# One warm matmul, one weight copy and the order of the last outputs, in a fused FFT and GEGLU kernel

## The chip, the cores and the metric

One core of one Trainium2 chip. The metric is the device time of one execution in microseconds (us). A "run" is one such execution; each run also has the span from its first to its last instruction and the mean clock that TensorE was granted (1.0 is full speed). The device time is about 2 us longer than the span (616.80 against 614.9 us in before's profiled run). Quoted times are medians of runs.

## The reference

```
x: [8, 3008, 256] float32;  w_gate, w_val: [256, 1536];  w_out: [1536, 256]
X = fft(fft(x, axis=1), axis=2).real          # over the sequence, then the 256 features
t = X.reshape(24064, 256)
g = t @ w_gate
out = (gelu(g) * (t @ w_val)) @ w_out         # exact gelu (erf), float32
```

## The kernel before

The feature FFT is folded into the weights on the chip (`make_w` multiplies the gate and value weights by DFT matrices into `W_sb`). The sequence FFT is two stages of small matmuls. Its real part is even in the sequence index up to the sign of an odd part O, so each position gives two outputs: sign 0 ("even": E + O) and sign 1 ("odd": E - O). Two copies of a weight serve this: O, and -2 O, which turns E + O in PSUM into E - O. Layer 1 and gelu make two products h per piece of 128 of the 1536 features; layer 2 multiplies the twelve pieces by `w_out`.

Part A sits in the opening. "Warm" matmuls on zeros keep TensorE busy while the first data is prepared:

```python
def warm(n):                                            # L843
    ps = psum("o")
    for _ in range(n):
        nc.tensor.matmul(ps[:, :], idle[:, 0:128], idle[:, :], start=True, stop=True)
# ... cut ...
s1(0, 2, 0)()                       # stage 1, pair by pair; each needs a fold by VectorE
s1(0, 2, 1)()
t_sin()
gelu_table()
warm(6)
fold_piece(5, 4)
s1(0, 1, 0)()
s1(0, 1, 1)()
fold_piece(0, 1)
fold_piece(1, 4)
s1(0, 3, 0)()
s1(0, 3, 1, "V")()
warm(1)
s1(0, 0, 0)()
s1(0, 0, 1, "V")()
```

Part B sits in `make_w`, which copies the product out of PSUM and then writes the -2 O copy on the engine named, by default the engine of the first copy:

```python
if m_engine == "P":
    nc.gpsimd.tensor_scalar(dst, W["gv"[i], "O"][:, f0 : f0 + n], keep2, None, op0=ALU.mult)
elif (m_engine or engine) == "A":
    nc.scalar.activation(dst, src, AF.Copy, scale=keep2)              # L475
else:
    nc.vector.tensor_scalar(dst, src, keep2, None, op0=ALU.mult)      # L477
# ... cut; the plan, slot 2 of the first chunk:
(2, make_w(0, 512, 512, (0,), "V")), (2, make_w(0, 512, 512, (1,))),
```

Part C sits in the last layer 2. Its chunk has 481 positions: four groups ("sub") of 128, 128, 128 and 97, each with two signs, so eight outputs of twelve matmuls each. Each output is copied out of PSUM into a tile `out_sb` of its own, and then stored in two transfers:

```python
def osb_tile():
    return work([128, 2, C], FP32, "osb", 3, "out_sb")          # three buffers rotate
# ... cut; l2_piece, in the last chunk:
osb = osb_tile()
if sign == 0:
    nc.vector.tensor_copy(osb[:m, 0, :], pso[:m, half])                  # L791
    store(b, ci, sub, 0, osb[:, 0, :], nc.sync)
else:
    nc.scalar.activation(osb[:m, 1, :], pso[:m, half], AF.Copy)          # L794
    store(b, ci, sub, 1, osb[:, 1, :], nc.scalar)
# ... cut; store(): the first of two transfers goes to the named queue, the second to SyncE's
(nc.sync if i else queue).dma_start(out=dst, in_=...)                    # L675
# ... cut; the order:
subs = [nsub - 1, *range(nsub - 1)] if last(ci) else range(nsub)
l2s = [l2_piece(ci, s, g, f) for s in subs for g in range(2) for f in range(0, NFC, L2P)]
```

## Time and profile before

| before | |
|---|---|
| time, three runs | 616.60, 616.64, 617.27 us |
| span and granted clock of the profiled run | 614.9 us, 0.997 |
| TensorE busy | 98% of the span |
| TensorE's share of the chain that ended last | 94% |

A profile line of the chain is "start, length, link". A line of the timeline is "start, busy time, engine, source line, operation, output<-inputs, count", and in brackets how long the engine had been idle and whose end released it.

### The profile page before, as it was taken

How to read it: one execution, taken by the hardware profiler on the slowest of the kernel's cores; microseconds unless marked ns; L12 is line 12 of the kernel's file. 1: busy time of each engine (PE TensorE's matmuls, PEld its weight loads, DVE VectorE, ACT ScalarE, POOL GpSimd, SP SyncE). 2: the span in 40 equal slices, each digit the busy share in tenths (PEclk: the TensorE clock that was granted, in tenths of full speed). 3: DMA queues.
4: the chain of work that ended last, by engine and by line, in shares of the span. 5: the costliest groups of instructions: out<-in, count | busy, mean ns of one | idle time of the engine just before them, and what ended most of it. 6: DMA issues, size and time to landing. Idle time of an engine off the chain costs nothing.

```text
span 614.9 us, 12747 instructions
## 1 busy us (share of the span) xinstructions
PE 605.4 (98%) x4181; PEld 406.9 (66%) x4229; DVE 577.3 (94%) x941; ACT 425.0 (69%) x824; POOL 508.9 (83%) x513
## 2 busy tenths in 40 slices
PE   8999999999999999999999999999999999999997
PEld 4466666666666666666666666666666666666666
DVE  8799999999999999999999999999999999999992
ACT  6888677777776777667766677666776676666661
POOL 8999899999987999789997899869997655565551
PEclk8999999999999999999999999999999999999999
DMA  9962834547253364532553344533213223111123
GB/s 175 200 137 57 237 95 117 141 116 189 80 144 92 100 163 119 140 100 58 157 150 94 106 107 107 146 102 100 64 49 77 62 87 78 42 46 47 37 51 83
DMA packets 52466, 65.40 MB, mean 106 GB/s; under 512 B 7629, under 2 KB 47278, under 8 KB 50004
## 3 DMA queue, kind: packets, MB, share of 16 engines
q1 hardware_dynamic: 45472, 49.03, 30.5%
q0 software_dynamic: 6608, 15.29, 11.7%
q8 instruction: 33, 0.54, 0.4%
q10 hardware_dynamic: 320, 0.26, 0.2%
q14 instruction: 33, 0.27, 0.2%
HBM read 39.65 MB, written 30.17 MB: 114 GB/s over the span
## 4 chain that ended last, share of the span: by engine, by line
PE 94%; DVE 2%; issue 1%; DMA 1%; ACT 1%; SPq 1%; POOL 0%; DVEq 0%; POOLq 0%; ACTq 0%
PE ps_o L778 39%; PE ps_g L681 29%; PE ps_v L681 20%; PE ps_dft L562 2%; PE ps_dft L598 2%; DMA out_dram<-out_sb 1%; PE ps_dft L451 1%; SPq L675 1%; PE ps_o L847 0%; PE ps_dft L542 0%; ACT gelu_sb L705 0%; ACT gelu_sb L714 0%; DVE v_sb L751 0%; POOL h_sb L753 0%; PE ps_dft L603 0%
## 5 line engine op out<-in xcount | busy, mean ns | idle before, releaser
L753 POOL TENSOR_TENSOR h_sb<-gelu_sb,v_sb 128x512 bf16<-128x512 bf16 (+1 forms) x280 | 319.9, 1147 | 87.0 <-DVE v_sb L751 79.0
L778 PE MATMUL ps_o<-Wo_sb,h_sb 128*128 128x256 bf16 (+1 forms) x2232 | 334.3, 272 | 0.0
L778 PEld LDWEIGHTS <-h_sb 128*128 128x128 bf16 (+1 forms) x2304 | 228.6, 100 | 111.2 <-POOL h_sb L753 1.0
L733 DVE SCALAR_TENSOR_TENSOR ve_sb<-EB_sb,yw,ps_v 128x512 f32<-128x512 bf16 (+1 forms) x280 | 206.3, 737 | 18.6 <-PE ps_v L681 16.6
L705 ACT ACTIVATE gelu_sb<-ps_g 128x512 bf16<-128x512 f32 (+1 forms) x288 | 169.3, 588 | 78.1 <-PE ps_g L681 62.9
L749 DVE TENSOR_TENSOR h_sb<-gelu_sb,ps_v 128x512 bf16<-128x512 bf16 (+1 forms) x280 | 190.0, 678 | 0.7
L681 PEld LDWEIGHTS <-W_sb 128*128 128x128 bf16 x1440 | 138.4, 98 | 78.0 <-issue 1.7
L751 DVE SCALAR_TENSOR_TENSOR v_sb<-ve_sb,ps_v 128x512 f32<-128x512 f32 (+1 forms) x280 | 187.4, 669 | 0.0
L714 ACT ACTIVATE gelu_sb<-ps_g 128x512 bf16<-128x512 f32 (+1 forms) x288 | 168.6, 585 | 0.0
L681 PE MATMUL ps_g<-O_sb,W_sb 128*128 128x512 bf16 (+1 forms) x530 | 159.1, 374 | 2.7 <-DVE O_sb L610 0.3
L681 PE MATMUL ps_g<-E_sb,W_sb 128*128 128x512 bf16 (+1 forms) x287 | 107.6, 375 | 0.7 <-ACT gelu_sb L714 0.5
L681 PE MATMUL ps_v<-O_sb,W_sb 128*128 128x512 bf16 (+1 forms) x288 | 108.0, 375 | 0.0
L681 PE MATMUL ps_v<-E_sb,W_sb 128*128 128x512 bf16 (+1 forms) x288 | 107.9, 375 | 0.0
L798 ACT ACTIVATE out_sb<-ps_o 128x512 f32<-128x512 f32 x92 | 55.0, 598 | 34.2 <-PE ps_o L778 34.1
L229 POOL TENSOR_TENSOR eo_sb<-ab_sb 94x512 bf16<-94x512 f32 (+1 forms) x70 | 77.7, 1112 | 0.4
L565 ACT ACTIVATE S_sb<-ps_dft 96x512 bf16<-96x512 f32 x56 | 33.2, 592 | 29.7 <-PE ps_dft L562 29.7
L222 POOL TENSOR_TENSOR ab_sb<-x_raw,x_raw 94x508 f32<-94x508 f32 (+1 forms) x30 | 33.0, 1101 | 0.0
L225 POOL TENSOR_TENSOR ab_sb<-x_raw,x_raw 94x508 f32<-94x508 f32 (+1 forms) x30 | 33.0, 1100 | 0.0
L562 PE MATMUL ps_dft<-eo_sb,G 94*96 94x256 bf16 x119 | 22.3, 272 | 0.0
L608 ACT ACTIVATE E_sb<-ps_dft 128x512 bf16<-128x512 f32 (+1 forms) x23 | 13.6, 590 | 12.0 <-PE ps_dft L598 12.0
L608 ACT ACTIVATE O_sb<-ps_dft 128x512 bf16<-128x512 f32 (+1 forms) x22 | 13.0, 590 | 11.6 <-PE ps_dft L598 11.1
L163 POOL DMA_INDIRECT x_raw<-in_x_dram,idx x18 | 17.2, 957 | 2.9 <-issue 0.8
(151 smaller groups left out, 207.6 us busy)
## 6 DMA issues: line engine op xcount, KB each, us to landing
out_dram<-out_sb SPq DMA_DIRECT2D x364, 64.0 KB
x_raw<-in_x_dram SPq DMA_DIRECT2D x10, 768.0 KB
Z_sb<-z SPq DMA_DIRECT2D x7, 768.0 KB
z<-S_sb SPq DMA_DIRECT2D x7, 576.0 KB
EB_sb<-yrow SPq DMA_DIRECT2D x6, 376.2 KB
z<-S_sb SPq DMA_DIRECT2D x7, 192.0 KB
x_raw<-in_x_dram SPq DMA_DIRECT2D x2, 640.0 KB
x_stage<-in_x_dram SPq DMA_DIRECT2D x1, 768.0 KB
```

What stands on the lines that cost most here:

```text
L229: eng.tensor_tensor(_sub(eo, [[C, nj], [1, 128]], j0 * C + g * 128), ab(0, 0, [[1, 128]]), ab(1, 0, [[1, 128]]), op=op)
L562: nc.tensor.matmul(ps[:96, q * C : (q + 1) * C], G[:, j, :], _sub(eo, [[1, C]], j * C), start=(j == js[0]), stop=(j == js[-1]))
L565: nc.scalar.activation(_sub(st["S"], [[1, 512]], (4 * jg + 2 * half) * C, part_num=96), ps[:96, :], AF.Copy)
L681: nc.tensor.matmul(ps[:, :n], W[nm, part][:, fs], src, start=start, stop=stop, **kw)
L705: nc.scalar.activation(gl[:, 0, :n], pg[:, :n], AF.Gelu)
L714: nc.scalar.activation(_sub(gl, [[-1, n]], TOK + n - 1), pg[:, :n], AF.Gelu)
L733: nc.vector.scalar_tensor_tensor(ve[:, :n], EB_bufs[b][:, c0 : c0 + n], yw[:, fc : fc + 1], pv[:, :n], op0=ALU.mult, op1=ALU.add)
L749: nc.vector.tensor_tensor(st["h"][:, fc, 0, :n], gl[:, 0, :n], pv[:, :n], op=ALU.mult)
L751: nc.vector.scalar_tensor_tensor(_sub(vv, [[-1, n]], n - 1), ve[:, :n], 2.0, pv[:, :n], op0=ALU.mult, op1=ALU.subtract)
L753: nc.gpsimd.tensor_tensor(st["h"][:, fc, 1, :n], gl[:, 1, :n], vv[:, :n], op=ALU.mult)
L778: nc.tensor.matmul(pso[:m, half], st["h"][:, fc, sign, h0 : h0 + m], Wo_sb[:, fc, :], start=(fc == 0 and not (first and sign)), stop=(fc = ...
L798: nc.scalar.activation(_sub(osb, [[1, 2 * C]], 0, part_num=m), pso[:m, :], AF.Copy)
```

## The change

Its intent: take three waits off TensorE at the two ends of the program. A drops the warm matmul that stands ahead of stage 1's last pair (and issues two weight copies in a slightly different place, which leaves every engine's own sequence as it was). B moves one -2 O copy from ScalarE, where two gelus wait behind it, to VectorE. C computes two even outputs first in the last layer 2, so that the first odd output no longer waits for GpSimd's last product.

```diff
-            subs = [nsub - 1, *range(nsub - 1)] if last(ci) else range(nsub)
-            l2s = [l2_piece(ci, s, g, f) for s in subs for g in range(2) for f in range(0, NFC, L2P)]
+            order = [(s, g) for s in range(nsub) for g in range(2)]
+            if last(ci):
+                order = [(nsub - 1, 0), (0, 0), (nsub - 1, 1), *order[1:-2]]
+            l2s = [l2_piece(ci, s, g, f) for s, g in order for f in range(0, NFC, L2P)]
 ...
-        warm(1)
         s1(0, 0, 0)()
 ...
-        copies.pop()()
         make_w(1, 0, 256, m_at=minus, m_engine="V", tag="v", copy_at=copies)()
+        copies[0]()
 ...
-        copies.pop()()
+        copies[1]()
 ...
-                (2, make_w(0, 512, 512, (0,), "V")), (2, make_w(0, 512, 512, (1,))),
+                (2, make_w(0, 512, 512, (0,), "V")), (2, make_w(0, 512, 512, (1,), m_engine="V")),
```

## The prediction

> **What bounds the kernel now.** I read the page's busy table first, then its chain of work that ended last, then the chain and timeline of two stretches where TensorE is not the only link: 13 to 26 us and 599 us to the end.
>
> ```profile
> PE 605.4 (98%) x4181; PEld 406.9 (66%) x4229; DVE 577.3 (94%) x941; ACT 425.0 (69%) x824; POOL 508.9 (83%) x513
> ...
> PE 94%; DVE 2%; issue 1%; DMA 1%; ACT 1%; SPq 1%; POOL 0%; DVEq 0%; POOLq 0%; ACTq 0%
> ```
>
> TensorE carries 94% of the chain. Start-to-start distances of its matmuls agree: between 45 and 599 us the time beyond each matmul's own cadence sums to about 1.8 us (leaving out doubled distances of one lone matmul each, which are missing records). So a microsecond taken from a TensorE stall before 45 us should move all that follows, to the end. The change touches none of the steady state, only the two ends. The chain of waits of 0 to 45 us:
>
> ```profile
> 13.21 0.40 PE ps_dft L520 x5
> 13.61 0.34 PE ps_o L847
> 13.96 0.17 PE ps_g L520 x4
> ...
> 22.48 0.88 PE ps_dft L451 x4
> 23.36 0.02 issue
> 23.38 0.60 ACT W_sb L459
> 23.98 0.58 ACT W_sb L475
> 24.56 0.49 ACT gelu_sb L705
> 25.05 0.50 ACT gelu_sb L714
> 25.54 0.04 issue
> 25.58 0.81 PE ps_g L681 x3
> ```
>
> Columns: start, length, link. The warm matmul (L847) is itself a link of 0.34 us. At 23.38 the chain leaves TensorE for four ScalarE instructions; the second, L475, is the -2 O copy of the weight that the change moves. The timeline at the end:
>
> ```profile
> 600.45 2.24 POOL L753 TENSOR_TENSOR h_sb<-gelu_sb,v_sb 128x481 bf16<-128x481 bf16 x2 [0.78 <-DVE v_sb L751]
> ...
> 602.74 7.89 PEld L778 LDWEIGHTS <-h_sb 128*97 128x97 bf16 x73 [0.55 <-POOL h_sb L753]
> 602.74 0.31 PE L778 MATMUL ps_dft<-Wo_sb,h_sb 128*97 128x256 bf16 x1 [0.30 <-POOL h_sb L753]
> ```
>
> The second output of the last layer 2 waits, with eleven of its twelve matmuls done, for the last product h of GpSimd.
>
> **What the Trainium skill says.**
> - "TensorE: Matmul & The Clock Gate", Part 1: the array's clock is halved or full, decided over a free-running window of 3413 ns; 512-column matmuls start 426.7 ns apart cold, about 216 ns warm. The trace agrees: the warm matmuls at 10.69, 11.11 and 11.54 us are 0.427 us apart, later ones 0.216, and its clock records give one stretch of 3.413 us at 0.5, from 10.33 to 13.74 us.
> - "ScalarE: Activation LUTs", What ACT_TABLE_LOAD costs: each [128,1] pointer operand adds about 93 ns to an ACTIVATE, and back-to-back ones overlap by about 93 ns. The trace agrees: the plain copy L459 took 0.597 us, L475 with its scale column 0.682, and L475 began 0.103 us before L459's end.
> - "DMA: Bandwidth & Descriptors", Why a DMA increments its semaphore by 16 and not by 1: the number of engines of a DMA is the largest number up to 16 that divides the slowest dimension, so 31 rows run on one engine. The trace agrees: the 31-row store, issued at 604.00, landed at 607.13 us, while the 64-row stores mostly take 1.9 to 2.1 us.
>
> **The change part by part.**
>
> *A, one warm matmul less.* VectorE's last fold (L225) ends at 13.415 us and stage 1's matmuls before it are just through, so the warm matmul fills no wait: it started at 13.412 and the first matmul of stage 1's last pair at 13.792, 0.380 later (the clock rose in between). Without it that pair starts at about 13.42. Its first five matmuls then run cold, 0.080 apart, instead of 0.042, so the last starts near 13.86 instead of 14.09. The gain shrinks further: the second copy of A (L528) needs VectorE, which works on the one before until 13.650 + 0.558 = 14.21. It started at 14.334, so it can start at 14.22, 0.11 earlier. The next TensorE link that waits on it is the matmul at 14.950 (released at 14.90). **A: about 0.1 us.** The order of instructions shows the moved weight copies change no engine's sequence; only three waits of TensorE on itself are new, for things long done.
>
> *B, -2 O in slot 2 on VectorE.* From the start of L475 (23.876) to the next ScalarE start (24.446) is 0.570 us. The matmul that waits at the end of this chain started at 25.583, 0.891 after the 512-column matmul before it; at the cadence of 0.216 the stall is 0.675. Without L475 gelu ends 0.570 earlier, so a stall of about 0.105 is left. Can the gelus start that early? The gate matmul that L705 needs started at 23.397 and took 0.376: 23.77, before 23.876. On VectorE the same instruction exists in slot 6 (L477, 0.751 us). It fits after the copy L461 (23.575 + 0.684 = 24.26), into the idle 0.82 us that stands there now; it ends near 24.95, and the product L728, at 25.077 so far, starts no later. It must also follow ScalarE's L459, done at 23.98. **B: 0.55 to 0.57 us, all on the path.**
>
> *C, two even outputs first.* Work is the same: 96 matmuls at 0.109 us. Now the last even product holds the start of the twelfth matmul to 600.933 (0.07 of wait, kept), and the last odd one holds another from 602.174 + 0.109 = 602.283 to 602.744: 0.46 us. A matmul after such a wait also cost 0.149 instead of 0.109. In the new order twelve matmuls (1.31 us) stand in between, and the odd output's twelfth comes near 601.08 + 23 x 0.109 = 603.6, after GpSimd's 602.70. **TensorE gains 0.50 us.** It reaches the end only if the stores follow. Three out_sb buffers rotate, so each copy needs the store three outputs back. My sums, with issues of 0.55 to 0.6 us on SyncE and landings of 2.05 us: the 31-row store moves from 604.0 to about 605.2 and lands near 608.3. That delays the sixth copy to about 608.4, where TensorE would let it go at 607.8. It delays no matmul. The fifth copy (607.42 now, held by that very store) goes at 606.7, its store lands by 609.8, and the eighth copy, the last, starts at TensorE's end: 610.45 instead of 610.95. **C: 0.45 us, less if the 31-row store pushes SyncE's queue.**
>
> Sum: 0.1 + 0.57 + 0.45 = 1.12 us, 0.18% of 616.64. Prediction **615.5 us**.
>
> **The rivals.**
> 1. *The tail turns store-bound and C comes to nothing.* For it: the last copy started at 610.952 when TensorE's output was ready at 610.91 and a store had landed at 610.97 by the record, so two chains end together; the 31-row store on one engine now sits behind two more. Against: that store's tile is needed only by copy six, and SyncE has about 0.2 us spare by my sums. If it held, the total gain would be 0.7 us: 615.95.
> 2. *VectorE becomes the link in slot 2.* For it: L477 is 0.751 us, longer than the 0.570 that ScalarE loses, and VectorE is 94% busy overall. Against: in slot 2 it sits idle 0.82 us, and these slots have two products an instance instead of three instructions. If L477 delayed the products, three ps_v buffers would absorb it. At worst B halves: 615.8.
> 3. *The clock.* The warm matmuls keep the window busy, and one less could leave TensorE cold for another window. For it: the window is free-running, so in other executions its edge falls elsewhere. Against: in this trace the pair of stage 1 takes the warm matmul's place at once, so the window stays full. If the clock is already full at this point, A gains nothing, since VectorE's fold is then waited for. If a cold window followed, from 13.7 to 17.1 us, the roughly 2 us of matmul cadence in it would double where they are on the path: up to 1.5 us lost, 617.0. I give that 5%.
>
> **Range and chances.** The three runs of before spread from 616.60 to 617.27, so a median may sit 0.3 us off. With A between 0 and 0.2, B 0.3 to 0.6 and C 0 to 0.5, gains lie between 0.3 and 1.3 us; adding the spread, 614.9 to 616.3 should hold it 8 times in 10. A 2% move would be 12.3 us; all stalls at the two ends together do not hold that much, and nothing in the steady state is touched. So within 2%: 0.99.
>
> **What would show it.**
> - A: stage 1's last pair starts at once behind the pair before; the matmul now at 14.950 comes 0.1 earlier. Wrong if a second stretch of half clock follows, or that matmul has not moved.
> - B: ScalarE goes from L459 straight to L705; the 0.891 us distance shrinks to about 0.32; L477 stands in VectorE's gap. Wrong if the matmul waits for VectorE instead.
> - C: no wait of TensorE for GpSimd in the last layer 2; the last copy starts 0.5 us earlier, measured from the last slot's end. Wrong if that copy waits for a store.
> - Whole: matmul starts around 300 us should be about 0.65 us earlier than before. If they are not, a wait in the first 45 us took back what B gave, and my claim that early gains pass through is wrong.

## More of the kernel before

The clock records of before have one stretch at half clock, 10.326 to 13.739 us; here are that stretch and the next. Columns: window, its length, TensorE's busy time and matmuls, granted clock, share of the DMA engines, GB/s.

```profile
10.33:13.74 3.41, 3.41 (x24) 0.50 1.21 167
13.74:17.15 3.41, 3.41 (x37) 1.00 1.19 151
```

TensorE had no idle time in the half-clock stretch, and the clock rose at its end.

## The result, and the profile after

| | before | after |
|---|---|---|
| runs | 616.60, 616.64, 616.80, 617.27 | 615.78, 616.22, 617.70, 617.94 |
| median | 616.72 | 616.96 |
| granted clock of after's runs, in the same order | | 0.999, 0.997, 0.994, 0.994 |

The ratio is 1.0001 (95% interval 0.9979 to 1.0023): no difference. A ratio here and below is the mean time of one kernel's fast runs over that of the other's of the same rounds, so it is not quite the ratio of the medians. By these eight runs the prediction of 615.5 (614.9 to 616.3) failed. The four runs of after fall into two pairs, 1.8 us apart, and the pair with the granted clock of 0.994 is the slow one. The profile was taken in a run of 0.994. Its head, its busy table and its chain by engine:

```profile
span 615.9 us, 12785 instructions
...
PE 607.3 (99%) x4228; PEld 407.4 (66%) x4228; DVE 577.6 (94%) x942; ACT 424.8 (69%) x823; POOL 508.3 (83%) x513
...
PE 97%; DMA 1%; POOL 1%; ACT 0%; DVE 0%; issue 0%; POOLq 0%; DVEq 0%
```

One instruction has left ScalarE (824 to 823), one has come to VectorE (941 to 942). VectorE and ScalarE have almost gone from the chain (in part because its opening now runs through a load), and still the span is 0.9 us longer. (TensorE's busy time is no help here: before's trace lacks some matmul records, 4181 against 4229 weight loads.)

To see where, I cut each profiled span at two places: the first matmul of the FFN (the first TensorE line L681), and the first matmul of the last layer 2 (the TensorE line L778 of 97 columns). The last column is the time between the first and the last matmul start of that layer 2.

| profiled run | start to first FFN matmul | to last layer 2 | to the end | span | TensorE in the last layer 2 |
|---|---|---|---|---|---|
| before | 17.32 | 582.34 | 15.27 | 614.93 | 10.98 |
| after | 19.14 | 581.87 | 14.85 | 615.86 | 10.48 |

The middle gained 0.47 and the end 0.42 us, and the opening lost 1.82. The chain of after through the opening:

```profile
4.84 7.17 DMA xb<-in_x_dram
...
12.67 0.50 PE ps_dft L520 x4
13.17 0.41 PE ps_g L520 x4
...
15.01 0.85 PE ps_o L451 x4
15.87 0.43 PE ps_dft L542 x2
```

and TensorE's busy time in the windows of its clock, as shown of before above:

```profile
11.07:14.49 3.42, 2.63 (x25) 0.50 1.34 178
14.49:17.90 3.41, 3.41 (x22) 0.50 1.20 182
```

Two things happened. The load of x that the second pair of stage 1 needs landed at 12.01 us (before: 11.16, by the same transfer's record), so that pair started at 12.67 instead of 11.96: 0.71 us lost. TensorE was idle for 0.79 us at this wait, the window from 11.07 held 2.63 us of work in 3.42, and the clock stayed at half for one window more, to 17.90. The idle time stands in TensorE's timeline, at the fold that waited for the load:

```profile
12.67 0.50 PE L520 MATMUL ps_dft<-G,eo_sb 94*128 94x96 bf16 x4 [0.79 <-DVE eo_sb L222]
```

In the second window, 256-column matmuls started 0.213 us apart instead of 0.109. From the second pair to the first FFN matmul it is 6.47 us in after and 5.36 in before: the other 1.11 us. Both events come before the code that the change touches: the removed warm matmul stood behind this pair. Whether they are chance or the change's doing is the first thing to test.

### The profile page after: what moved, and what is told of

Same layout as the page of the kernel before. It is cut to its first block, busy times and chain, and to the rows that moved or that the text cites. A ratio compares the mean times of both kernels' runs of the same rounds, so it can differ in the third digit from the quotient of the medians.

```text
span 615.9 us, 12785 instructions
## 1 busy us (share of the span) xinstructions
PE 607.3 (99%) x4228; PEld 407.4 (66%) x4228; DVE 577.6 (94%) x942; ACT 424.8 (69%) x823; POOL 508.3 (83%) x513
## 3 DMA queue, kind: packets, MB, share of 16 engines
q0 software_dynamic: 6608, 15.29, 11.5%
## 4 chain that ended last, share of the span: by engine, by line
PE 97%; DMA 1%; POOL 1%; ACT 0%; DVE 0%; issue 0%; POOLq 0%; DVEq 0%
PE ps_o L778 40%; PE ps_g L681 30%; PE ps_v L681 20%; PE ps_dft L562 2%; PE ps_dft L598 2%; DMA xb<-in_x_dram 1%; PE ps_dft L451 1%; PE ps_v L778 0%; PE ps_g L778 0%; PE ps_dft L778 0%; PE ps_dft L542 0%; POOL xb L163 0%; PE ps_dft L603 0%; PE ps_dft L520 0%; PE ps_o L451 0%
## 5 line engine op out<-in xcount | busy, mean ns | idle before, releaser
L778 PE MATMUL ps_o<-Wo_sb,h_sb 128*128 128x256 bf16 (+1 forms) x2232 | 334.2, 272 | 0.0
L778 PEld LDWEIGHTS <-h_sb 128*128 128x128 bf16 (+1 forms) x2304 | 228.7, 100 | 110.4 <-POOL h_sb L753 0.2
L705 ACT ACTIVATE gelu_sb<-ps_g 128x512 bf16<-128x512 f32 (+1 forms) x288 | 169.3, 588 | 78.4 <-PE ps_g L681 73.6
L681 PEld LDWEIGHTS <-W_sb 128*128 128x128 bf16 x1440 | 138.4, 98 | 77.7 <-issue 1.4
L681 PE MATMUL ps_g<-O_sb,W_sb 128*128 128x512 bf16 (+1 forms) x576 | 169.0, 375 | 0.2 <-DVE O_sb L610 0.2
L681 PE MATMUL ps_g<-E_sb,W_sb 128*128 128x512 bf16 (+1 forms) x288 | 107.9, 375 | 0.2
L681 PE MATMUL ps_v<-O_sb,W_sb 128*128 128x512 bf16 (+1 forms) x288 | 108.0, 375 | 0.0
L681 PE MATMUL ps_v<-E_sb,W_sb 128*128 128x512 bf16 (+1 forms) x288 | 108.0, 375 | 0.0
```

The lines of the kernel that those rows point to most:

```text
L681: nc.tensor.matmul(ps[:, :n], W[nm, part][:, fs], src, start=start, stop=stop, **kw)
L705: nc.scalar.activation(gl[:, 0, :n], pg[:, :n], AF.Gelu)
L778: nc.tensor.matmul(pso[:m, half], st["h"][:, fc, sign, h0 : h0 + m], Wo_sb[:, fc, :], start=(fc == 0 and not (first and sign)), stop=(fc = ...
```

## The experiments

Theories before the runs: (1) the opening's loss is a draw that either kernel can have, and the change gains close to what was predicted; (2) the missing warm matmul leaves the clock low, so A costs more than B and C gain; (3) the tail is bound by its stores and C comes to nothing; (4) VectorE gives back what B takes from ScalarE. All runs gave correct results, and all count as fast (none is over 1.5% above the fastest of its kernel). Each kernel had six runs, and before eleven runs on the same chip.

| kernel | median (range) | before | ratio (95%) | runs at clock 0.994 or less |
|---|---|---|---|---|
| e1 after again | 616.09 (615.51-616.25) | 617.19 | 0.9979 (0.9966-0.9992) | 0 of 6 |
| e2 A alone | 617.24 (616.93-617.27) | 617.19 | 0.9997 (0.9984-1.001) | 0 |
| e3 B alone | 616.36 (615.98-618.22) | 617.19 | 0.9993 (0.9977-1.001) | 1 |
| e4 C alone | 616.96 (616.50-618.68) | 617.19 | 0.9997 (0.9981-1.0013) | 1 |
| e5 B and C | 616.11 (615.68-617.33) | 616.66 | 0.9986 (0.9969-1.0004) | 0 |
| e6 after, four out_sb | 615.58 (615.46-617.47) | 616.66 | 0.9974 (0.9958-0.9991) | 1 |
| e7 after, one store on ScalarE's queue | 615.54 (615.14-617.21) | 616.66 | 0.9978 (0.9959-0.9996) | 1 |
| e8 after, without warm(6) | 616.91 (616.22-618.06) | 616.66 | 0.9999 (0.998-1.0017) | 5 |
| e9 e6 and e7 together | 615.44 (615.29-617.52) | 616.90 | 0.9978 (0.996-0.9996) | 1 |
| e10 e9 with warm(9) | 616.32 (616.12-617.56) | 616.90 | 0.999 (0.9974-1.0006) | 0 |
| e11 after, third time | 616.09 (615.68-618.27) | 616.90 | 0.9981 (0.9965-0.9996) | 1 |
| e12 before with B and four out_sb | 616.11 (615.72-617.90) | 617.25 | 0.9982 (0.9966-0.9998) | 1 |

The same cut of one profiled run of each:

| profiled run | to first FFN matmul | to last layer 2 | to the end | half-clock windows in the opening |
|---|---|---|---|---|
| before | 17.32 | 582.34 | 15.27 | 1 |
| after | 19.14 | 581.87 | 14.85 | 2 |
| e1 | 17.02 | 581.72 | 15.00 | 1 |
| e2 | 17.34 | 582.35 | 15.45 | 0 |
| e3 | 17.15 | 581.72 | 15.29 | 1 |
| e4 | 17.09 | 583.22 | 15.67 | 0 |
| e5 | 17.03 | 581.71 | 15.10 | 0 |
| e6 | 19.28 | 581.59 | 14.76 | 2 |
| e7 | 17.09 | 581.71 | 14.77 | 1 |
| e8 | 18.21 | 581.72 | 14.87 | 2 |
| e9 | 17.22 | 581.56 | 14.78 | 1 |
| e10 | 18.02 | 581.55 | 14.77 | 1 |
| e11 | 18.62 | 582.04 | 15.75 | 2 |
| e12 | 17.31 | 581.58 | 15.31 | 1 |

### The changed kernel again, twice: e1 and e11

No edit.

> The changed kernel once more, with each run's mean granted clock beside its time. Theory 1 (a draw of the opening): times fall into groups by the clock: near 615.6 us at 0.999, 616.1 at 0.997, 617.7 at 0.994, and the kernel before shows the same three groups, each 0.5 to 1 us higher at the same clock. Theory 2 (the missing warm matmul leaves the clock low): this kernel has 0.994 in at least half its runs, the kernel before in none.

> The changed kernel a third time, on this chip, for the size of its gain in the same rounds as the repaired one: 616.1 us, 0.8 to 1.1 us below the kernel before in the medians, and one run in eight or so above 617.2 with clock 0.994.

Measured: 616.09 us both times, on two chips, and both intervals lie below 1. Before ran at 617.19 and 616.90 beside them. In all, after has 16 runs: 615.51 to 618.27, median 616.12. Before has 48: 616.27 to 619.40, median 617.08. So the change gains about 0.96 us by these medians, and the result, "no difference", was a draw of four. TensorE's timeline in the profiled run of e1, with no late load and one half-clock window:

```profile
9.98 2.66 PE L850 MATMUL ps_o<-gelu_sb 128*128 128x512 bf16 x6
12.47 0.34 PE L520 MATMUL ps_dft<-G,eo_sb 94*128 94x96 bf16 x4
14.54 0.39 PE L542 MATMUL ps_dft<-II,A_sb 128*128 128x256 bf16 x2 [0.29 <-ACT A_sb L526]
17.02 0.38 PE L681 MATMUL ps_g<-E_sb,W_sb 128*128 128x512 bf16 x1
```

Against the same kernel's run on record the first FFN matmul comes 2.12 us earlier (17.02 against 19.14), with the same code. Theory 1 holds for the opening. Of its three groups only one shows: after's runs at 0.994 or less are slow, but those at 0.997 (615.51 to 616.89) and those at 0.998 or more (615.78 to 616.25) don't separate.

### One part alone: e2, e3, e4

e2 keeps only A, e3 only B, e4 only C; the diff of each is its part of the diff above.

> Only the warm matmul taken out, and the weight copies reordered. Theory 1: 616.6 us, within 0.2 of the kernel before at the same clock; clock 0.994 no more often than the kernel before has it. Theory 2: clock 0.994 in at least half the runs, and those near 618.7 us.

> Only the -2 O copy of slot 2 on VectorE. Both theories: 0.5 to 0.6 us below the kernel before at the same clock, and the distance of the matmul that waited for the gelu falls from 0.89 to about 0.32 us. A third theory, that VectorE gives it back in slots 2 and 3, has less than 0.2 us.

> Only the new order of the last layer 2. From the changed kernel's trace: 0.35 us below the kernel before at the same clock (last copy 0.5 us earlier, but the SyncE queue 0.15 us later behind the 31-row store). If the tail is bound by the stores: 0.0 to 0.1 us.

**A** gave nothing in the medians: 617.24 against 617.19 us. The profiles tell more, because its worth depends on where the clock's window falls. Where the clock is full before stage 1's last pairs, nothing is gained: e1 without the matmul and e3 with it both need 4.55 us from stage 1's second pair to the first FFN matmul, and in e1 TensorE waits for the copy of A_sb instead (the 0.29 us in its lines). In e7, whose opening is after's, the half-clock window stood where it stood in before, at 10.33 to 13.74 us. Before, then e7:

```profile
13.41 0.54 PE L847 MATMUL ps_o<-gelu_sb 128*128 128x512 bf16 x1
13.79 0.34 PE L520 MATMUL ps_g<-G,eo_sb 94*128 94x96 bf16 x4
14.71 0.52 PE L542 MATMUL ps_dft<-II,A_sb 128*128 128x256 bf16 x2
```

```profile
13.39 0.50 PE L520 MATMUL ps_g<-G,eo_sb 94*128 94x96 bf16 x4
14.47 0.52 PE L542 MATMUL ps_dft<-II,A_sb 128*128 128x256 bf16 x2
```

From the second pair to the first FFN matmul e7 needs 5.15 us, before 5.36, and e12, which keeps the matmul and has nearly the same window (10.27 to 13.68), 5.30. So A is worth some 0.15 to 0.2 us there, by these three profiles.

**B** worked nearly as predicted: the middle shrank from 582.34 to 581.72 us, 0.62, and the same 581.7 stands in e1, e3, e5, e7 and e8. Before, a gate matmul waited for gelu behind L475:

```profile
23.88 0.68 ACT L475 ACTIVATE W_sb<-ps_dft,keep 128x512 bf16<-128x512 f32 x1
24.45 0.60 ACT L705 ACTIVATE gelu_sb<-ps_g 128x512 bf16<-128x512 f32 x1
25.58 0.38 PE L681 MATMUL ps_g<-E_sb,W_sb 128*128 128x512 bf16 x1 [0.51 <-ACT gelu_sb L714]
```

and after (the whole stretch comes 1.4 us later because of the opening; L459 is the instruction that stood ahead of L475):

```profile
25.35 0.60 ACT L459 ACTIVATE W_sb<-ps_dft 128x512 bf16<-128x512 f32 x1 [0.62 <-PE ps_dft L451]
25.85 0.59 ACT L705 ACTIVATE gelu_sb<-ps_g 128x512 bf16<-128x512 f32 x1
26.15 0.74 DVE L477 TENSOR_SCALAR W_sb<-ps_dft,keep 128x512 bf16<-128x512 f32 x1
26.98 0.38 PE L681 MATMUL ps_g<-E_sb,W_sb 128*128 128x512 bf16 x1
27.08 0.60 ACT L459 ACTIVATE W_sb<-ps_dft 128x512 bf16<-128x512 f32 x1
27.73 0.39 PE L681 MATMUL ps_v<-E_sb,W_sb 128*128 128x512 bf16 x1
```

L705 follows L459 with nothing between, L477 stands on VectorE beside it, and no matmul here waits for VectorE: theory 4 falls. But not all of the saving at the waiting matmul (0.575 us) is kept. Three matmuls later, the one at 27.73 starts 0.11 us late, after ScalarE's next weight copy, which ended at 27.68. With both set to 0 at the first FFN matmul, e3 is 0.49 us ahead of before at 50 us and 0.51 at 300 us. The rest of the 0.62 is made of pauses of about 0.15 us inside a group of matmuls (at 270.5 and 566.7 us in before, at 212.8 us in e7), whose cause no profile here shows.

**C** took 0.50 us from TensorE (10.98 to 10.48 in every profile with the new order), but e4's end took 15.67 us, longer than before's 15.27. Its middle is 583.22 instead of 582.35 mainly for another reason, seen in no other profile here: TensorE waited 0.62 us (from start to start) for a load of the stage-1 results:

```profile
72.60 4.61 DMA Z_sb<-z
77.21 0.04 issue
77.26 0.36 PE ps_dft L634
```

This transfer took 4.2 to 4.3 us in before, after and e1. It looks like a second kind of draw, seen once.

### The warm matmul kept: e5

```diff
         s1(0, 3, 1, "V")()
+        warm(1)
         s1(0, 0, 0)()
```

with the old places of the two copies; B and C stay.

> The changed kernel with the one warm matmul and the old order of copies put back. If that matmul is worth nothing (the run with it alone removed measured 0.9997 of the kernel before), this is as fast as the changed kernel within 0.2 us: about 616.1, and about 1 us below the kernel before. If taking it out gained the predicted 0.1 us or cost a half-clock window now and then, this differs from the changed kernel by more than 0.3 us.

Measured: 616.11 us, the same as after's 616.12 from 16 runs. They were run at other times. Against before of its own call the gain is 0.55 us, where about 1 was expected, and the interval (0.9969 to 1.0004) takes in no gain. Theory 2 has no support in this median: one warm matmul more or less at this place is worth nothing that six runs can see.

### The stores of the last outputs: e6, e7, e9, e12

With three buffers and the new order, the profiles of after, e1, e4, e5, e8 and e11 need 14.85, 15.00, 15.67, 15.10, 14.87 and 15.75 us from the first matmul of the last layer 2 to the end, mean 15.21. The old order with three buffers (before, e2, e3) needs 15.27, 15.45 and 15.29, mean 15.34. TensorE's 0.50 us reach the end as 0.13 on average, and since the six profiles spread over 0.9 us, that mean alone can't be told from nothing. (By the medians, C alone is 0.23 us faster than before, and e1 0.27 faster than B alone.) Take off TensorE's own stretch: before needs 4.29 us more (15.27 - 10.98), the six 4.37 to 5.27. The copies out of PSUM in e1 show why:

```profile
606.54 0.42 DVE L791 COPY out_sb<-ps_v 128x256 f32<-128x256 f32 x1 [4.45 <-DMA out_dram<-out_sb]
609.67 0.38 ACT L794 ACTIVATE out_sb<-ps_g 128x256 f32<-128x256 f32 x1 [1.14 <-DMA out_dram<-out_sb]
```

TensorE had finished the first of these two outputs at about 605.6 us. The copy waited until 606.54 for its buffer, whose store landed at 606.42. The last copy waited for a store that landed at 609.56. The store of 606.42 is the second transfer of the early even output: SyncE took 1.37 us to issue it, where such an issue takes about 0.5 to 0.6 (from the trace's record of SyncE's issues: 603.56 to 604.93). In after it took 1.23, in e4 1.51, in e5 1.29, in e11 1.57, in e8 0.60; with the old order and three buffers none took over 0.97. SyncE's sixteen issues of the end (shortest, median and longest in ns), in before and then in e1:

```profile
L675 SPq DMA_DIRECT2D out_dram<-out_sb x16: 235/536/712, 600.1 to 611.4; - x16
L675 SPq DMA_DIRECT2D out_dram<-out_sb x16: 382/513/1369, 599.2 to 610.4; - x16
```

e6 gives the outputs a fourth buffer, e7 sends one of the two transfers of the early output to ScalarE's queue, e9 does both, and e12 has the old order with the fourth buffer:

```diff
-        return work([128, 2, C], FP32, "osb", 3, "out_sb")                   # e6, e9, e12
+        return work([128, 2, C], FP32, "osb", 4, "out_sb")
 ...                                           (and the one other tile that shares "osb")
-                        store(b, ci, sub, 0, osb[:, 0, :], nc.sync)          # e7, e9
+                        store(b, ci, sub, 0, osb[:, 0, :], nc.sync if sub else nc.scalar)
```

> The changed kernel with four out_sb buffers in place of three. If the tail is held by stores through the rotation of buffers: copies five, six and eight start when TensorE is done, the stretch from the last layer 2's first matmul to the end falls from 14.9 to 15.0 us (changed kernel) to about 14.6, and the time by 0.2 to 0.4 us. If SyncE's issues alone hold it: the copies start earlier but the end stays at 14.9.

> The changed kernel with the first store of the early even output (sub 0) issued by ScalarE in place of SyncE. If SyncE's queue, whose fifth to eighth issues stand back to back and whose eighth took 1.2 to 1.5 us, is what delays the fifth copy by 1 us: that issue falls to 0.6 us, the fifth copy starts 0.6 to 1 us earlier after TensorE, and the end comes 0.1 to 0.3 us earlier. If the long issue has another cause: it stays above 1 us and the time does not move.

> The changed kernel with both repairs of the tail: four out_sb buffers, and the early even output's first store on ScalarE's queue. Each alone measured about 0.5 us below the changed kernel's median of 616.1. If both cut the same wait (copies held by stores): together no more than either, 615.4 to 615.6. If the one cuts the wait for buffers and the other SyncE's queue: 615.2, and the stretch from the last layer 2's first matmul to the end about 14.6 us against 14.77 in each alone.

> The kernel before with the -2 O copy on VectorE and four out_sb buffers, in the old order of the last layer 2 (against the run with four buffers and the new order: tail 14.76 us). If the new order is worth its 0.5 us of TensorE time once stores hold no copy: tail 15.2 to 15.3 us, and the time 0.4 to 0.6 us above that run, near 616.1. If the buffers alone bring the gain and the order nothing: tail 14.8 us, time near 615.6.

With either repair the end takes 14.76 to 14.78 us in all four profiles that have one (e6, e7, e9, e10). In e9 the same two copies wait only for TensorE:

```profile
605.64 0.42 DVE L791 COPY out_sb<-ps_v 128x256 f32<-128x256 f32 x1 [3.51 <-PE ps_v L778]
609.56 0.38 ACT L794 ACTIVATE out_sb<-ps_g 128x256 f32<-128x256 f32 x1 [2.24 <-PE ps_g L778]
```

The old order with four buffers (e12) still takes 15.31, with TensorE's wait for GpSimd in place. So at the end the buffer alone is worth nothing, the order alone about 0.13, and both together 15.34 - 14.77 = 0.57 us. (In the middle, the four profiles with a fourth buffer are 0.13 to 0.17 us shorter than those at 581.7; e9 lacks the pause at 212.8 us.)

The times agree for the repairs: e6 and e7 ran 0.53 and 0.57 us faster than e5 (B and C with three buffers), and both together (e9) gain no more than either. For e12 they don't decide: its 616.11 is 0.53 above e6, but in another call, where before was 0.59 slower too, and against before of its own call it gains 1.14 us, e6 1.08. That the new order is worth anything with four buffers rests on the ends of the profiles.

Theory 3 was right in its mechanism: the stores held back most of C. It was the stores' buffers and SyncE's issues, not the bandwidth, since one more buffer or one store moved is enough. Why SyncE's one issue stretches to over a microsecond isn't settled. It overlaps in time with an issue of ScalarE's, and e7, which moved the store ahead of it to the other queue, had 0.47. The fourth buffer doesn't remove it (e6: 1.24), and the old order with four buffers has one too (e12: 1.18). But an overlap alone does not stretch an issue: in e1 at 608.55 us both queues issue together, in 0.47 and 0.50.

### The clock of the opening: e8, e10

e8 takes the six warm matmuls ahead of stage 1's second pair away; e10 makes them nine, on top of e9.

```diff
-        warm(6)             # e8: removed;  e10: warm(9)
```

> The changed kernel without the six warm matmuls that fill the wait ahead of stage 1's second pair. This provokes on purpose what two of the first four runs of the changed kernel showed. If a half-clock window between 11 and 18 us is what makes the slow runs: most runs have clock 0.994 to 0.997 and 617 to 618 us, and the first feed-forward matmul starts at 18.5 to 19.2 us in the profile in place of 17.0 to 17.3. If the slow runs come from late transfers alone: 616.1 us, start near 17.1.

> The same with nine warm matmuls in place of six ahead of stage 1's second pair. If idle TensorE time there is what makes a second half-clock window: no run at 0.994 or below, and the median falls by no more than 0.2 us; in runs whose clock is half at that point the three add up to 0.6 us. If the extra matmuls delay stage 1 in most runs: median 0.3 to 0.6 us above the run without them.

e8 provokes what after's run had: the clock was 0.994 or less in 5 of 6 runs, against 3 of 16 for after, and the median rose by 0.8 us against after's 616.12. They were run at other times. (It was milder than expected: three of six runs above 617, and the first FFN matmul at 18.21 us.) Its two half-clock windows:

```profile
9.44:12.86 3.42, 1.12 (x12) 0.81 (x13) 3.14 (x12) 3.33 (x8) 3.42 (x6) 0.50 1.16 172
12.86:16.27 3.41, 3.41 (x31) 2.86 (x29) 2.45 (x8) 2.07 (x5) 3.11 (x5) 0.50 1.22 163
```

(The busy times are of TensorE, its weight loads, VectorE, ScalarE and GpSimd.) TensorE worked 1.12 us of the first window, and the next one stayed at half. So idle time of TensorE in a half-clock window is a cause of the second window, not its companion. The other profiles agree: the window after was at half where the first held 1.12 (e8), 2.63 (after), 2.97 (e11) or 3.12 us (e6) of work, and at full where it held 3.09 (e3), 3.22 (e1) or all 3.41 (before, e7, e9, e10, e12). In after, e6 and e11 the idle time was a wait for a fold of VectorE ahead of stage 1's first or second pair, before the place of the change. The draws of the opening are these: the half clock began at 8.99 to 11.62 us, and not at all in e2, e4 and e5; and the load of x landed at 11.58 to 12.01 us in the four profiles with two half-clock windows and at 10.78 to 11.38 in the other ten (in e11 the idle time lies ahead of its landing, so there it isn't the cause).

The clock number tells the two kinds of run apart, since two windows of 3.413 us at half cost 6.83 x 0.5 / 615 = 0.0056 of the mean. After's 3 runs at 0.994 or less took 617.70, 617.94 and 618.27 us, the median of its other 13 is 616.07. Before's 3 took 618.37, 618.59 and 619.40 among 45 runs with a clock noted, the median of the other 42 is 617.03. Over all kernels with the six warm matmuls, 6 of 40 runs without the one warm matmul and 6 of 69 with it were at 0.994 or less: too few to tell them apart.

e10 had no such run in six, but nine warm matmuls in a half-clock window delay stage 1 itself: the first FFN matmul came at 18.02 us instead of e9's 17.22, and the median was 616.32 instead of 615.44, more than the 0.3 to 0.6 expected. The six of the kernel are the better bet.

**The version that beats both** is e9: 615.44 us, ratio 0.9978 to before, with an end of 14.78 us. Against after (e11) it gains 0.65 us by the medians, though the six runs of each overlap.

## Why the prediction was wrong, point by point

- **The whole.** By the result it was wrong, 616.96 against a range up to 616.3. The median of all 16 runs of after, 616.12, lies in the range, 0.6 us above the predicted 615.5. Two steps failed: the spread, and the size of C.
- **The spread, failed.** "The three runs of before spread from 616.60 to 617.27, so a median may sit 0.3 us off." Three runs did not show the spread. Before's 48 runs reach from 616.27 to 619.40, and their median is 617.08, 0.44 above the base of 616.64 that the gain was subtracted from. After's 16 span 2.8 us, and two of the four had a second half-clock window, so that median was 0.84 off. Of the 16 runs 12 lie in the predicted range; a median of four falls in it when at least three do, some 0.74 by chance (0.75 to the fourth, plus 4 x 0.75 cubed x 0.25). So the record was an unlucky draw, of a range somewhat too narrow. The range also falls short of its own terms: the least gain of 0.3 and the spread of 0.3 make 616.64 at the top, not 616.3.
- **Rival 3, the clock.** What it said of the clock and its price was right: a half-clock window to 17.9 us instead of 17.1, 1.11 us lost from it in the profiled run, where "up to 1.5 us lost, 617.0" was written. The cause was another: it was filed as a consequence of the missing warm matmul at 5%, where a late load had left TensorE idle before that place, a draw that either kernel has (3 of 16 runs of after, 3 of 45 of before).
- **A, right in kind.** "A between 0 and 0.2" is what the profiles show: 0.15 to 0.2 us with the window where the prediction had it (e7), nothing with a full clock, as rival 3 foresaw, though TensorE then waits for a copy of A_sb and not for "VectorE's fold". The medians don't show it. In e7 the matmul of 14.950 came at 14.716, 0.23 earlier and not 0.1: VectorE's second copy began 0.08 us before the one before it ended, where the sum had it wait for that end.
- **B, right, with some luck.** 0.55 to 0.57 predicted, 0.62 measured in the middle of e1, e3, e5 and e7. "All on the path" was not quite so: 0.49 is left behind the wait for ScalarE's next copy, and the pauses elsewhere happen to add 0.13. The distance of 0.891 us before the waiting matmul became 0.316, where about 0.32 was predicted; VectorE's L477 took 0.74 (0.751 predicted). The check on the whole, at 300 us, holds in part: e3 is 0.51 us ahead of before there, measured from the first FFN matmul, and after is behind, since the opening took back what B gave. Early gains do pass through to the last layer 2.
- **C, failed in size.** TensorE's 0.50 us was right to the hundredth. "C: 0.45 us, less if the 31-row store pushes SyncE's queue" measured 0.13 on average. The step that failed is "SyncE has about 0.2 us spare by my sums", with "issues of 0.55 to 0.6 us on SyncE": one issue took 1.2 to 1.6 us in five of the six profiles with this order and three buffers. The "fifth copy", expected at 606.7 where before had it at 607.42, went 0.94 us after TensorE was done in e1, and the last copy, expected at TensorE's end, waited for a store in e1 and in e4. Rival 1's 615.95 was nearest to the middle of after's runs, by luck, as its base was 0.44 too low. Its reading of before's end was off: a store that landed at 610.97 can't have held a copy that started at 610.952. The store that freed this copy's buffer had landed at 610.44, and TensorE's output came last; so the stores had about 0.5 us to spare in before, and the new order used it up.
- **The sum.** Predicted 1.12; the profiles show 0 to 0.2 for A, 0.62 and 0.13, so 0.75 to 0.95; the medians of 16 and 48 runs differ by 0.96. That they meet proves little: the medians of before in its four calls alone range from 616.66 to 617.25. What makes before's slowest runs slow at a full clock (7 of its 42 runs above 0.994 took over 618 us) isn't settled; a late load as in e4 is one candidate that a profile showed.

## What to carry to other kernels

A gain below the spread of single runs can't be read from three or four of them: first ask what the draws of the opening (a late load, a clock window) cost, cut the span there, and compare the parts behind it. A saving on the busiest engine at the end of a program reaches the end only if the copies and stores behind it have buffers to spare, so change the order and the buffers together. And a warm-up matmul is worth what it keeps of a clock window: the single one cost 0.15 to 0.2 us where it ran at half clock; with six the clock was mostly kept, without them it was lost in 5 of 6 runs, and nine delayed the real work by 0.8 us.

## What the Trainium skill lacked or had wrong

- "TensorE: Matmul & The Clock Gate", Part 1, says that the clock rises after a busy window, but not how busy. Here windows with 3.09, 3.22 and 3.41 us of TensorE work in 3.41 raised it, and windows with 1.12, 2.63, 2.97 and 3.12 did not. So the bound lies near 3.1 us, nine tenths, by the profile's busy time, which is modelled. Nor does it say how little work lets the clock fall, and no clean bound comes out here: windows with 1.51 (after) and 1.62 us (e6) lost the full clock, windows with 1.94 to 2.02 us (e2, e4, e5) kept it, but nine with 2.42 to 2.93 us, 1.2 of them in one-column matmuls, lost it too. The same part says that "the ramp penalty is <1% of a typical kernel span"; that agrees (1.1 us of 616, 0.2%), but here it was as large as the whole change.
- "DMA: Bandwidth & Descriptors", Why a DMA increments its semaphore by 16 and not by 1, has the rule by which 31 rows go on one engine, but no time for such a store: 3.13 us from issue to landing in before, against about 2.05 for a store of 64 rows.
- No page gives a length for the stretched issue: SyncE's second store of one output took 1.23 to 1.57 us to issue in six profiles with the new order (e6 among them), against 0.5 to 0.6 otherwise, without a wait on a semaphore that the profile shows. Whether it waited for something that the two queues share isn't settled here.
